# Attention and gated feed-forward on one core: three quarters of the layer norm on GpSimd, value tiles later, and the first products reordered

## The chip, the cores and the metric

The kernel runs on one core of one Trainium2 chip. The metric is device time in microseconds, the median of several runs; profiles show one execution each.

## The reference

The kernel computes a layer norm of `x` (2048 tokens of 512 values), and adds to `x` an attention block and a gated feed-forward block, both of the normalised tokens. There are 32 heads of 16 values.

```python
xn = _layernorm(x, axis=-1)
return x + _A_ref(xn, A_wqkv, A_wo) + _B_ref(xn, B_w1, B_w3, B_w2)
# _A_ref
    qkv = (x @ wqkv).reshape(B, S, 3, H, Dh) ...      # H = 32, Dh = 16
    scores = jnp.einsum("bhqd,bhkd->bhqk", q, k) * (Dh ** -0.5)
    p = _softmax(scores, axis=-1)
    o = jnp.einsum("bhqk,bhkd->bhqd", p, v)
    return o.transpose(...).reshape(B, S, D) @ wo
# _B_ref
    h = _silu(x @ w1) * (x @ w3)
    return h @ w2
```

## The kernel before

The 2048 queries are cut into four blocks of 512, the 32 heads into eight groups of four. A block and a group make one query tile `QT` (three buffers). Each is worked in units of 256 queries; the very last 256 queries are two units of 128. There are 65 units.

Each unit goes twice over its scores.

- The first pass finds the maximum of each query and head. TensorE makes a *product*: two matmuls (line 775, `p1_cand`) of 128 queries against 512 keys for two heads, which fill two of the PSUM banks 0 to 3. VectorE takes the maximum of 1024 columns (line 796, a *reduction*) into `part`. A unit of 256 queries has 16 products: four key blocks `kc`, two query tiles, two head pairs, key blocks outermost. Two bank pairs alternate, so TensorE can be at most two products ahead of VectorE. In all there are 1024 products. When a unit's last reduction is in, `final_max` (line 837) makes the negative maximum `negm`.
- GpSimd writes `negm` into two rows of `Z` (lines 813 and 815). For units in `FAST_AUG` the query tile is then built again by matmuls that include these rows (`tile_QT2`, copied by ScalarE at line 605). For all others three DMAs on SP carry the rows into `QT` (line 834, then line 830 twice). A unit that has this is "ready" (`AUG`).
- The second pass makes the scores again, transposed, with the maximum subtracted (line 904), and ScalarE takes the exponential of 512 columns (line 922) into a slot of `PT`. A unit of 256 queries has 32 of them, one of 128 queries 16. `tile_PV` multiplies by the values `Vaug`, whose 17th column of ones yields the sum; ScalarE copies the result to `U` (line 986), and a chain of DMAs and GpSimd operations divides by the sum (lines 1005 to 1031).

The feed-forward tiles and the output tiles are placed into what TensorE has left between these.

**The head.** `x` is fetched in four groups of four token tiles of 128 tokens (`load_x`, line 389) into `PT`, the weights `wk`, `wq` and `wv` by `load_w` (line 393) into `hT`. For each token group `ln_chunk` has VectorE take the statistics (lines 466 and 469) and GpSimd the inverse deviation `lnr` (line 474, and a power at line 476). The first group is normalised on VectorE (line 489). For the other three GpSimd also makes `lnb` = -mean times `lnr` (lines 480 and 482), and ScalarE normalises (line 494). A normalised tile lies in one of four slots of `osb`, is transposed on TensorE (line 518) and copied by ScalarE to `xnT` (line 524). With all four tiles of a group there, `tile_KT` makes 512 keys of the first head group (16 matmuls, copied at line 539), and `tile_QT` the first queries (copied at line 582). `tile_V` makes the values of one token tile (copied at line 558); there are 16 of these. The weights are spread out ("pads") with gaps of zeros: `wk` on GpSimd (lines 412 and 417), `wq` on ScalarE (lines 422 and 427). GpSimd also writes the ones of `Vaug` (line 440) and clears `wo` (line 442).

**What sets the order.** The order of instructions on each engine is fixed when the kernel is built. A planner keeps queues per engine (`dveq` and `redq` for VectorE, `expq` and `miscq` for ScalarE, `poolq` for GpSimd, `spq` for SP), a planned cost of each item (`occ`, `lat`) and the planned time at which each engine is free, and again and again emits the item that can start first. `pred` holds an item back until something is in `done`. TensorE tiles wait in `head_tiles`, `crit` (sorted by `need`, the number of the product before which the tile is wanted), `ffn` and `outs`; `assign` and `choose` give them one of the PSUM banks 4 to 7. `fill_cand` inserts matmuls whose result is not used where the planned load of TensorE in the last 2.3 us falls under a threshold. On the chip each engine follows the emitted order and waits on semaphores.

Of the kernel before, what the change touches and what calls it, by code (L numbers as in the profile page):

```python
# [225 lines left out]
def _build(nc, A_x, A_wqkv, A_wo, B_w1, B_w3, B_w2, out):  # L226
# [27 lines left out]
    for qc in range(NQC):  # L254
        for g in range(NG):
            last = qc == NQC - 1 and g == NG - 1
            for (q0, nq) in ([(0, 256), (256, 128), (384, 128)] if last else [(0, 256), (256, 256)]):
                units.append((qc, g, q0, nq))
    NU = len(units)
    FAST_AUG = {0, NU - 3, NU - 2, NU - 1}  # L260
    FAST_PV = {NU - 3, NU - 2, NU - 1}
# [4 lines left out]
    def sb(name, shape, dt):  # L266
        return ctx.enter_context(nc.sbuf_tensor(name, list(shape), dt))

    with ctx:
# [7 lines left out]
        lnr = sb("lnr", [128, NT], FP32)  # L277
        lnb = sb("lnb", [128, NT], FP32)
        lnt = sb("lnt", [128, NT], FP32)
# [112 lines left out]
        def load_w(dst, w, off):  # L392
            P.dma(lambda e: e.dma_start(dst, wqkv_v[:, :, off * D:(off + 1) * D]), writes=STG_KEYS[w], lat=5.0)
        load_x(0)
        load_w(wkst, "wk", 1)
        load_w(wqst, "wq", 0)
        load_x(1)
        load_x(2)
# [34 lines left out]
        for c in range(DC):  # L433
            poolq["pad"].append(_Item(pad_rest(wk, wkst, c), STG_KEYS["wk"], [("wk", 1 + c)], 0.62,
                                      pred=lambda: ("KT", 0, 0) in done))
        WK_KEYS = [("wkpad",)] + [("wk", i) for i in range(DC + 1)] + ON0_KEYS
# [3 lines left out]
        poolq["pad"].append(_Item(lambda e: e.memset(Vaug[:, :, :, 16:17], 1.0), [],  # L440
                                  [("Vone",)], 2.2))
        poolq["pad"].append(_Item(lambda e: e.memset(wo[:, :, :], 0.0), [], [("wo",)], 3.5,
# [18 lines left out]
        def ln_chunk(gi):  # L461
            tl = range(gi * XG, (gi + 1) * XG)
            sl_ = slice(gi * XG, (gi + 1) * XG)
            MVK = [("mv", t) for t in tl]
            for t in tl:
                dveq.append(_Item(lambda e, t=t: e.bn_stats(stats[:, t, :], x_sb[:, t, :]),
                                  [("PT", t)], [("st", t)], 0.6, 0.7))
            for t in tl:
                dveq.append(_Item(lambda e, t=t: e.bn_aggr(mv[:, t, :], stats[:, t, :]), [("st", t)], [("mv", t)],
                                  0.075, 0.2))  # L470

            def coef(op):
# [3 lines left out]
                q.append(_Item(lambda e: e.tensor_tensor(lnr[:, sl_], lnt[:, sl_], mhalf[:, sl_], ALU.pow),  # L476
                               [("lnt", gi), ("mhalf",)], [("lnr", gi)], 1.05, 1.15,
                               cb=norm if gi == 0 else None))
                if gi > 0:
                    q.append(_Item(lambda e: e.tensor_tensor(lnt[:, sl_], mv[:, sl_, 0], lnr[:, sl_], ALU.mult),  # L480
                                   [("lnr", gi)] + MVK, [("lnt", gi)], 0.25, 0.35))
                    q.append(_Item(lambda e: e.tensor_scalar(lnb[:, sl_], lnt[:, sl_], -1.0, 0.0, ALU.mult, ALU.add),
                                   [("lnt", gi)], [("lnb", gi)], 0.25, 0.35, cb=norm))

            def norm(op):
                for t in tl:
                    xs = t % 4
                    if gi == 0:
                        dveq.insert(t - gi * XG, _Item(lambda e, t=t, xs=xs: e.tensor_scalar(
                            xn_sb[:, xs, :], x_sb[:, t, :], mv[:, t, 0:1], lnr[:, t:t + 1], ALU.subtract, ALU.mult),  # L490
                            [("PT", t), ("lnr", gi), ("mv", t)], [("osb", xs)], 0.34, 0.45,
                            cb=lambda op, t=t: tr_ready(t)))
                    else:
                        miscq.append(_Item(lambda e, t=t, xs=xs: e.activation(  # L494
                            xn_sb[:, xs, :], x_sb[:, t, :], ACTF.Identity, scale=lnr[:, t:t + 1], bias=lnb[:, t:t + 1]),
                            [("PT", t), ("lnr", gi), ("lnb", gi)], [("osb", xs)], 0.55, 0.65,
                            cb=lambda op, t=t: tr_ready(t), pred=lambda t=t: ("xnT", t - 4) in done))
            dveq[-1].cb = coef
# [51 lines left out]
        def tile_V(t, need=None):  # L550
# [6 lines left out]
            def evac(bk):  # L557
                return [_Item(lambda e: e.activation(Vaug[:, t, :, 0:16],
                                                     bank(bk).rearrange("p (h d) -> p h d", d=16), ACTF.Identity),
                              [("ps", bk)], [("V", t)], _c_act(512), cb=lambda op: done.add(("V", t)))]  # L560
            return _Tile("V%d" % t, groups, evac, need=need, pred=lambda: ("xnT", t) in done)

# [179 lines left out]
        for u in range(NU):  # L742
            p1_first.append(len(p1))
            p1 += p1_list(u)
        NP1 = len(p1)
        p1_n = [0]
# [4 lines left out]
        def p1_cand():  # L751
# [19 lines left out]
            def emit():  # L771
# [328 lines left out]
        def assign():  # L1100
# [305 lines left out]
```

## Time and profile before

| what | value |
|---|---|
| median of three runs | 1257.77 us (1254.86 to 1262.67) |
| the profiled execution | 1256.76 us, its span 1255.0 us |
| VectorE busy | 1200.6 us, 96% |
| ScalarE busy | 1203.5 us, 96% |
| TensorE matmul busy | 1171.5 us, 93% |
| GpSimd busy | 358.7 us, 29% |
| normalising on ScalarE (line 494) | 12 operations, 8.9 us |
| value copies on ScalarE (line 558) | 16 operations, 9.4 us |
| first reduction | starts at 19.15 us |
| first exponential | starts at 51.83 us |
| last reduction | ends near 1215.2 us |
| last exponentials | 55 after the last query tile, ending near 1249.3 us |

Busy time is the time in which an engine runs at least one instruction. Consecutive instructions of one engine overlap a little, so the mean length of a group is above its busy time divided by its count. In the rows of groups the numbers behind the first bar are busy time in us and the mean length in ns; behind the second bar stands the time for which the engine was idle just before, and what ended it. A line number such as L456 can be that of a helper that makes many kinds of matmuls; the names of the tiles tell them apart.

### The profile page before, as it was taken

Reading aid. Unit: us, or ns where it says so; the run is one execution under the profiler, and the core shown is the slowest. Engines: PE = TensorE matmul, PEld = TensorE weight load, DVE = VectorE, ACT = ScalarE, POOL = GpSimd, SP = SyncE. Lnnn points to the kernel's source line nnn. Section 1 sums busy time; section 2 is a strip of 40 time slices with the busy share of each in tenths; the row PEclk is TensorE's granted clock in tenths of the full one; section 3 lists DMA queues with packets and bytes.
Section 4 is the critical chain, followed back from the end, with each engine's and each line's share of the span. In section 5 each row is a group of like instructions: output and inputs, shape, how many; then the busy total and the mean of one; then the engine's idle time right before and its main releaser. Section 6 shows DMA issues by size and latency. Waiting matters only on the chain.

```text
span 1255.0 us, 39328 instructions
## 1 busy us (share of the span) xinstructions
PE 1171.5 (93%) x16989; PEld 431.4 (34%) x16989; DVE 1200.6 (96%) x1141; ACT 1203.5 (96%) x2413; POOL 358.7 (29%) x453
## 2 busy tenths in 40 slices
PE   5999999999999999999999999999999999989997
PEld 2333333333333333333333333333333333333334
DVE  6999999999999999999999999999999999999972
ACT  6799999999999999999999999999999999999997
POOL 4023232232321133324322123333332115454110
PEclk9999999999999999999999999999999999998989
DMA  8010110111011011111110111111110112120000
GB/s 226 2 26 17 23 22 18 24 19 27 17 19 28 20 36 23 26 25 28 28 23 20 28 34 25 28 20 23 28 28 17 27 36 42 34 45 7 11 5 21
DMA packets 112845, 36.27 MB, mean 29 GB/s; under 512 B 98232, under 2 KB 112672, under 8 KB 112672
## 3 DMA queue, kind: packets, MB, share of 16 engines
q1 hardware_dynamic: 112672, 33.76, 12.6%
q8 instruction: 133, 2.18, 0.7%
q14 instruction: 40, 0.33, 0.1%
HBM read 22.81 MB, written 2.10 MB: 20 GB/s over the span
## 4 chain that ended last, share of the span: by engine, by line
PE 49%; ACT 48%; issue 1%; DVE 1%; DMA 1%; SPq 0%; ACTq 0%; POOL 0%
ACT PT L922 39%; PE ps L456 28%; PE ps L904 12%; PE ps L775 8%; ACT th L644 2%; ACT zg L646 2%; ACT ub L650 2%; ACT QT L582 1%; ACT KT L539 1%; DMA PT<-in_A_x_dram 1%; ACT U L986 1%; DVE part L796 0%; ACT osb L494 0%; ACT osb L707 0%; DVE R L975 0%
## 5 line engine op out<-in xcount | busy, mean ns | idle before, releaser
L796 DVE TENSOR_REDUCE part<-ps 128x2 f32<-128x1024 f32 x1024 | 1176.7, 1216 | 18.4 <-PE ps L775 10.1
L922 ACT ACTIVATE PT<-ps 128x512 bf16<-128x512 f32 x2048 | 1068.7, 636 | 24.8 <-PE ps L904 14.7
L904 PE MATMUL ps<-QT,KT 32*128 32x256 bf16 (+1 forms) x4160 | 565.1, 272 | 16.2 <-ACT QT L582 0.7
L775 PE MATMUL ps<-KT,QT 32*128 32x512 bf16 x2048 | 433.4, 385 | 2.0 <-DVE part L796 1.5
L904 PEld LDWEIGHTS ps<-QT,KT 32*128 32x128 bf16 x4160 | 182.1, 92 | 292.7 <-ACT PT L922 184.8
L1009 POOL TENSOR_TENSOR Rc<-Lc,mone 128x8 f32<-128x8 f32 x62 | 101.5, 1637 | 366.4 <-DMA Lc<-U 366.3
L456 PE MATMUL ps<-PT,Vaug 128*17 128x256 bf16 (+1 forms) x4160 | 178.5, 276 | 4.8 <-ACT PT L922 1.2
L456 PE MATMUL ps<-xnT,w 128*32 128x512 bf16 x1792 | 140.2, 384 | 25.8 <-ACT zg L646 21.0
L775 PEld LDWEIGHTS ps<-KT,QT 32*128 32x128 bf16 x2048 | 111.2, 91 | 145.4 <-issue 94.7
L456 PE MATMUL ps<-xnT,ident 128*32 128x512 bf16 x1732 | 138.8, 385 | 10.9 <-DVE osb L732 0.2
L456 PEld LDWEIGHTS ps<-PT,Vaug 128*17 128x17 bf16 x4160 | 83.4, 90 | 87.7 <-issue 65.0
L631 POOL TENSOR_TENSOR a<-zg,ub 128x512 f32<-128x512 bf16 x56 | 64.6, 1154 | 101.1 <-ACT ub L650 100.7
L813 POOL TENSOR_SCALAR Z<-negm 128x8 bf16<-128x8 f32 x64 | 14.7, 230 | 202.4 <-DVE negm L837 202.4
L633 POOL TENSOR_TENSOR hT<-a,t 128x512 bf16<-128x512 f32 x56 | 71.2, 1272 | 3.4
L456 PEld LDWEIGHTS ps<-xnT,w 128*32 128x32 bf16 x1792 | 39.3, 94 | 92.4 <-issue 74.9
L456 PE MATMUL ps<-w,hT 128*32 128x512 bf16 x896 | 70.6, 384 | 0.0
L456 PEld LDWEIGHTS ps<-xnT,ident 128*32 128x32 bf16 x1732 | 34.5, 94 | 83.3 <-ACT PT L922 70.1
L629 POOL TENSOR_SCALAR t<-th 128x512 f32<-128x512 bf16 x56 | 34.9, 623 | 55.6 <-ACT th L644 55.0
L456 PE MATMUL ps<-xnT,wq 128*32 128x512 bf16 (+2 forms) x576 | 43.2, 376 | 0.9 <-ACT zg L646 0.3
L456 PE MATMUL ps<-xnT,wk_on 128*32 128x512 bf16 x512 | 41.4, 400 | 1.7 <-ACT xnT L524 0.8
L1031 POOL TENSOR_TENSOR wk_on<-U,R 128x256 bf16<-128x256 f32 x30 | 21.9, 728 | 70.2 <-DMA R<-Rrow 69.9
L1031 POOL TENSOR_TENSOR on_b<-U,R 128x256 bf16<-128x256 f32 x32 | 23.3, 727 | 54.7 <-DMA R<-Rrow 54.7
(75 smaller groups left out, 432.1 us busy)
## 6 DMA issues: line engine op xcount, KB each, us to landing
w<-in_B_w_dram SPq DMA_DIRECT2D x112, 128.0 KB
R<-Rrow SPq DMA_DIRECT2D x248, 16.0 KB
PT<-in_A_x_dram SPq DMA_DIRECT2D x4, 512.0 KB
xr<-in_A_x_dram SPq DMA_DIRECT2D x16, 128.0 KB
out_dram<-osb SPq DMA_DIRECT2D x16, 128.0 KB
QT<-Zs SPq DMA_DIRECT2D x122, 2.0 KB
w<-in_B_w_dram SPq DMA_DIRECT2D x1, 1792.0 KB
hT<-in_A_wqkv_dram SPq DMA_DIRECT2D x3, 512.0 KB
```

The lines of the kernel that those rows point to most:

```text
L456: ins = e.matmul(bank(bk)[32 * i:32 * i + m, c0:c0 + ncols], make_lhsT(i), rhs_ap(i), start=start, stop=stop, tile_position=(0, 32 * i), **kw)
L629: q.append(_Item(lambda e: e.tensor_scalar(t1[:, :], th[:, ss, :], 1.0, 1.0, ALU.mult, ALU.add), [("th", ss)], [("t1",)], 0.62, 0.72))
L631: q.append(_Item(lambda e: e.tensor_tensor(a32[:, :], zg[:, ss, :], ub[:, ss, :], ALU.mult), [("zg", ss), ("ub", ss)], [("a32",)], 1.1, 1.25))
L633: q.append(_Item(lambda e: e.tensor_tensor(hT[:, fc, :], a32[:, :], t1[:, :], ALU.mult), [("a32",), ("t1",)], [("hT", fc)], 1.25, 1.35, cb ...
L644: return [_Item(lambda e: e.activation(th[:, ss, :], bank(bk), ACTF.Tanh, scale=0.5), [("ps", bk)], [("th", ss)], _c_act(512), cb=part_don ...
L646: _Item(lambda e: e.activation(zg[:, ss, :], bank(bk), ACTF.Identity, scale=0.5), [("ps", bk)], [("zg", ss)], _c_act(512), cb=part_done, n ...
L775: ins = e.matmul(bank(2 * sl + i), QT[32 * j:32 * j + 32, qs, q * 128:(q + 1) * 128], KT[32 * j:32 * j + 32, g, kc * 512:(kc + 1) * 512], ...
L796: redq.append(_Item(lambda e: e.tensor_reduce(part[:, par, qt, 2 * pair:2 * pair + 2, kc], ps[:, sl * 1024:(sl + 1) * 1024].rearrange("p ( ...
L904: ins = e.matmul(bank(b)[:, i * nq:(i + 1) * nq], KT[32 * j:32 * j + 32, g, (k0 + i) * 128:(k0 + i + 1) * 128], QT[32 * j:32 * j + 32, qs, ...
L922: expq.append(_Item(lambda e: e.activation(PT[:, sl, :], bank(b), ACTF.Exp, scale=SCALE), [("ps", b)], [("PT", sl)], _c_act(512), cb=cb))
L1009: poolq["nrm"].append(_Item(lambda e: e.tensor_tensor(Rc[:, pp, 0:nl], Lc[:, pp, 0:nl], mone[:, 0:nl], ALU.pow), [("Lc", pp), ("mone",)], ...
L1031: poolq["nrm"].append(_Item(lambda e: e.tensor_tensor(onorm[ob][:, g, q0:q0 + nq], U[:, us, 0:nq], R[:, pp, 0:nq], ALU.mult), [("U", us)] ...
```

## The change

- The first 256 queries of the first head group become two units of 128, and both are in `FAST_AUG`. There are now 66 units. The 16 products of these two units are put into this order: key block 0 for both units, key block 1 for both, then blocks 2 and 3 for the first unit, then for the second. A counter per unit (`p1_left`) tells when a unit's last reduction is in.
- `x` group 1 is fetched second, ahead of `wk` and `wq`.
- Token groups 1 to 3 are normalised on GpSimd, in the form that VectorE has for group 0: two per-partition scalars, subtract and multiply. `lnb` and its two operations are gone.
- Value tiles wait for the fourth key block of the first head group (`("KT", 0, NQC - 1)`). The rest of the `wq` pads waits for the same, the rest of the `wk` pads and the ones of `Vaug` for the last normalised tile. `tile_PV` waits for the last value tile.
- The `need` numbers of the query, key and value tiles change, and so do the conditions in `assign` and `fill_cand`.

```diff
@@ units
-            for (q0, nq) in ([(0, 256), (256, 128), (384, 128)] if last else [(0, 256), (256, 256)]):
+            first = qc == 0 and g == 0
+            for (q0, nq) in ([(0, 256), (256, 128), (384, 128)] if last else
+                             [(0, 128), (128, 128), (256, 256)] if first else [(0, 256), (256, 256)]):
...
-    FAST_AUG = {0, NU - 3, NU - 2, NU - 1}
+    FAST_AUG = {0, 1, NU - 3, NU - 2, NU - 1}
@@ loads
         load_x(0)
+        load_x(1)
         load_w(wkst, "wk", 1)
         load_w(wqst, "wq", 0)
-        load_x(1)
@@ pads of wk, ones of Vaug
-                                      pred=lambda: ("KT", 0, 0) in done))
+                                      pred=lambda: ("xn", NT - 1) in done))
...
-                                  [("Vone",)], 2.2))
+                                  [("Vone",)], 2.2, pred=lambda: ("xn", NT - 1) in done))
@@ ln_chunk, coef
-                               cb=norm if gi == 0 else None))
-                if gi > 0:
-                    q.append(_Item(lambda e: e.tensor_tensor(lnt[:, sl_], mv[:, sl_, 0], lnr[:, sl_], ALU.mult),
...
-                    q.append(_Item(lambda e: e.tensor_scalar(lnb[:, sl_], lnt[:, sl_], -1.0, 0.0, ALU.mult, ALU.add),
...
+                               [("lnt", gi), ("mhalf",)], [("lnr", gi)], 1.05, 1.15, cb=norm))
@@ ln_chunk, norm
+                    it = _Item(lambda e, t=t, xs=xs: e.tensor_scalar(
+                        xn_sb[:, xs, :], x_sb[:, t, :], mv[:, t, 0:1], lnr[:, t:t + 1], ALU.subtract, ALU.mult),
+                        [("PT", t), ("lnr", gi), ("mv", t)], [("osb", xs)], 0.34, 0.45,
+                        cb=lambda op, t=t: tr_ready(t))
                     if gi == 0:
...
+                        dveq.insert(t - gi * XG, it)
                     else:
-                        miscq.append(_Item(lambda e, t=t, xs=xs: e.activation(
-                            xn_sb[:, xs, :], x_sb[:, t, :], ACTF.Identity, scale=lnr[:, t:t + 1], bias=lnb[:, t:t + 1]),
...
+                        it.occ = 0.8
+                        it.lat = 0.9
+                        it.pred = lambda t=t: ("xnT", t - 4) in done
+                        poolq["ln"].append(it)
@@ tile_V
-            return _Tile("V%d" % t, groups, evac, need=need, pred=lambda: ("xnT", t) in done)
+            return _Tile("V%d" % t, groups, evac, need=need, pred=lambda: ("KT", 0, NQC - 1) in done)
@@ order of products
+        p1[0:16] = [b for kcs, us in (((0,), (0, 1)), ((1,), (0, 1)), ((2, 3), (0,)), ((2, 3), (1,)))
+                    for u in us for kc in kcs for b in p1_list(u) if b[2] == kc]
+        p1_left = [8 * units[u][3] // 128 for u in range(NU)]
...
-                    if red_n[0] == NP1 or p1[red_n[0]][0] != u:
+                    p1_left[u] -= 1
+                    if p1_left[u] == 0:
@@ due numbers
-            crit.append(tile_QT(ug, need=p1_first[2 * ug]))
+            crit.append(tile_QT(ug, need=32 * ug if ug > 1 else 20))
...
-                crit.append(tile_KT(g, sc, need=p1_first[2 * g] + 4 * sc))
+                crit.append(tile_KT(g, sc, need=32 * g + 4 * sc if g > 1 else 21 + 4 * sc))
...
-            crit.append(tile_V(t, need=24 + t))
+            crit.append(tile_V(t, need=12 + t))
@@ pv_ready
+            if ("V", NT - 1) not in done:
+                return False
@@ assign
-            if ("AUG", 0) not in done and p1_n[0] > 0 and not head_tiles:
+            if p1_left[0] > 1 and p1_n[0] > 0 and not head_tiles:
@@ fill_cand
-            if head_tiles or p1_n[0] < 48 or pv_u[0] >= NU or not low_load(P.free["pe"]):
+            if ("QT", 0) not in done or pv_u[0] >= NU or not low_load(P.free["pe"]):
@@ rest of the pads of wq
-                               pred=lambda: ("QT", 0) in done))
+                               pred=lambda: ("KT", 0, NQC - 1) in done))
```

More of the change, by code (lines that the diff above doesn't have):

```diff
@@ L277, in _build @@
         lnr = sb("lnr", [128, NT], FP32)
-        lnb = sb("lnb", [128, NT], FP32)
         lnt = sb("lnt", [128, NT], FP32)
@@ L476, in coef @@
                 q.append(_Item(lambda e: e.tensor_tensor(lnr[:, sl_], lnt[:, sl_], mhalf[:, sl_], ALU.pow),
-                               [("lnt", gi), ("mhalf",)], [("lnr", gi)], 1.05, 1.15,
-                               cb=norm if gi == 0 else None))
-                if gi > 0:
-                    q.append(_Item(lambda e: e.tensor_tensor(lnt[:, sl_], mv[:, sl_, 0], lnr[:, sl_], ALU.mult),
-                                   [("lnr", gi)] + MVK, [("lnt", gi)], 0.25, 0.35))
-                    q.append(_Item(lambda e: e.tensor_scalar(lnb[:, sl_], lnt[:, sl_], -1.0, 0.0, ALU.mult, ALU.add),
-                                   [("lnt", gi)], [("lnb", gi)], 0.25, 0.35, cb=norm))
+                               [("lnt", gi), ("mhalf",)], [("lnr", gi)], 1.05, 1.15, cb=norm))
             def norm(op):
@@ L487, in norm @@
                     xs = t % 4
+                    it = _Item(lambda e, t=t, xs=xs: e.tensor_scalar(
+                        xn_sb[:, xs, :], x_sb[:, t, :], mv[:, t, 0:1], lnr[:, t:t + 1], ALU.subtract, ALU.mult),
+                        [("PT", t), ("lnr", gi), ("mv", t)], [("osb", xs)], 0.34, 0.45,
+                        cb=lambda op, t=t: tr_ready(t))
                     if gi == 0:
[L489 to L492, printed above, removed]
-                    else:
-                        miscq.append(_Item(lambda e, t=t, xs=xs: e.activation(
-                            xn_sb[:, xs, :], x_sb[:, t, :], ACTF.Identity, scale=lnr[:, t:t + 1], bias=lnb[:, t:t + 1]),
-                            [("PT", t), ("lnr", gi), ("lnb", gi)], [("osb", xs)], 0.55, 0.65,
-                            cb=lambda op, t=t: tr_ready(t), pred=lambda t=t: ("xnT", t - 4) in done))
+                        dveq.insert(t - gi * XG, it)
+                    else:
+                        it.occ = 0.8
+                        it.lat = 0.9
+                        it.pred = lambda t=t: ("xnT", t - 4) in done
+                        poolq["ln"].append(it)
             dveq[-1].cb = coef
```

## The prediction

> **What bounds the kernel now.** I read the page first, then busy time by stretch, then the timelines of VectorE and ScalarE over the first 75 us, TensorE's over the first 53, and the last 60 us.
>
> ```profile
> PE 1171.5 (93%) x16989; PEld 431.4 (34%) x16989; DVE 1200.6 (96%) x1141; ACT 1203.5 (96%) x2413; POOL 358.7 (29%) x453
> ...
> L796 DVE TENSOR_REDUCE part<-ps 128x2 f32<-128x1024 f32 x1024 | 1176.7, 1216 | 18.4 <-PE ps L775 10.1
> L922 ACT ACTIVATE PT<-ps 128x512 bf16<-128x512 f32 x2048 | 1068.7, 636 | 24.8 <-PE ps L904 14.7
> ```
>
> Two engines are full at once: VectorE by 1024 reductions (L796), ScalarE by 2048 exponentials (L922). The stretches show where they are not (us, then busy us and count of PE, PEld, DVE, ACT, POOL; then the granted clock, the DMA share and GB/s):
>
> ```profile
> 19.00:33.20 14.20, 11.37 (x132) 4.91 (x132) 4.81 (x4) 14.20 (x26) 7.51 (x8) 0.76 0.53 119
> 33.20:51.83 18.63, 18.61 (x260) 6.78 (x257) 18.62 (x18) 10.58 (x20) 0.48 (x2) 1.00 0.01 3
> 51.83:73.00 21.17, 20.77 (x282) 7.13 (x278) 21.17 (x20) 21.05 (x42) 0.47 (x2) 1.00 0.07 16
> 110.00:400.00 290.00, 275.54 (x3922) 98.95 (x3924) 288.32 (x267) 286.55 (x579) 80.00 (x99) 1.00 0.11 21
> ```
>
> Between 19 and 33 us VectorE works 4.8 of 14.2 us while ScalarE has no gap: ScalarE holds up the head there. VectorE's timeline (start, length, count):
>
> ```profile
> 19.15 2.36 DVE L796 TENSOR_REDUCE part<-ps 128x2 f32<-128x1024 f32 x2 [0.19 <-PE ps L775]
> 22.51 1.23 DVE L796 TENSOR_REDUCE part<-ps 128x2 f32<-128x1024 f32 x1 [1.00 <-PE ps L775]
> 24.67 1.23 DVE L796 TENSOR_REDUCE part<-ps 128x2 f32<-128x1024 f32 x1 [0.93 <-PE ps L775]
> 33.20 14.80 DVE L796 TENSOR_REDUCE part<-ps 128x2 f32<-128x1024 f32 x13 [7.31 <-PE ps L775]
> 47.92 0.17 DVE L837 TENSOR_REDUCE negm<-part 128x8 f32<-128x32 f32 x1
> 48.02 18.18 DVE L796 TENSOR_REDUCE part<-ps 128x2 f32<-128x1024 f32 x16
> 66.12 0.17 DVE L837 TENSOR_REDUCE negm<-part 128x8 f32<-128x32 f32 x1
> ```
>
> The fifth reduction needs keys of the second token group (L539), and these come after twelve normalisations (L494, 8.9 us) and four value tiles (L558) on ScalarE. From 33.2 us on reductions follow each other at 14.80/13 = 1.14 us. The 33rd ends at 66.12.
>
> **Only the head can move.** I compared the order in which the two programs' instructions stand. From the 409th product (a pair of L775 matmuls feeding one reduction) and the 751st exponential on, every engine has the same instructions in the same order, the tail with its 55 last exponentials included. So the gain is how much earlier the two full engines arrive there, and VectorE cannot arrive earlier by more than it idles before.
>
> **The change part by part.**
>
> *Loads.* Token group 1 is fetched second. By the old landings (5.15, 6.70, 8.15, 9.65 us: first reader of each fetch) it lands at 6.7, wk at 8.15, wq at 9.65. GpSimd does the wk pad first: 8.15 + 0.41 + 0.20 (L474) + 1.02 (L476) + gaps = 9.9, so the first normalisation starts 0.35 earlier than at 10.26. Statistics end at 18.6, not 18.95; first reduction at 18.8. wq's pad at 9.65 + 0.42 stays ahead of its matmuls near 15.
>
> *Normalising on GpSimd.* ScalarE loses 8.9 us. GpSimd gains twelve 512-element operations, which no row shows; nearest are:
>
> ```profile
> L629 POOL TENSOR_SCALAR t<-th 128x512 f32<-128x512 bf16 x56 | 34.9, 623 | 55.6 <-ACT th L644 55.0
> L633 POOL TENSOR_TENSOR hT<-a,t 128x512 bf16<-128x512 f32 x56 | 71.2, 1272 | 3.4
> ```
>
> One tensor input costs 0.62 (0.57 for 448 in L417), two cost 1.15 to 1.27. It reads one tensor and two per-partition scalars, so I take 0.65 and keep 0.57 and 1.27. A group then takes 0.2 + 1.0 + 0.15 + 4 x 0.65 = 4.0 us, below the 4.56 of the four reductions it must stay ahead of. Normalising would run from 14.8 to about 25.4. Then pads 4 x 0.57, ones 2.38 (L440) and the clearing of wo 3.51 (L442) end at 33.8, before the first maximum at about 35.6, which GpSimd must pass on (L813); that cover is 1.8 us, gone at 0.80 per normalisation. At 1.27 group 3 ends at 17.5 + 12 x 1.27 = 32.7, its keys exist 2.8 later (transpose, xnT 0.6, KT matmuls 0.98, KT copy 0.7), at 35.5, and VectorE, which would need them at 32.1, loses 3.4. The Trainium skill (GPSIMD Engine Reference, section 3.1) says 512 elements take about 769 ns in the best loop and that elementwise work belongs on VectorE; here L489 shows 0.34 on VectorE against 0.62. By 0.77 a group takes 4.4 us, still below 4.56, and the sum stays.
>
> *Value tiles wait, units of 128, products in key order.* Of the first 16 products four need group 0 only, four group 1. Ideal: 18.8 + 33 x 1.137 + 0.1 for one more L837 = 56.4, so 9.7 earlier than 66.12. What is late instead: TensorE. These rows show two rates:
>
> ```profile
> 26.55 2.01 PE L518 MATMUL ps<-ident,osb 128*128 128x128 bf16 x12 [1.60 <-ACT osb L494]
> 28.49 1.90 PE L456 MATMUL ps<-xnT,wk_on 128*32 128x512 bf16 x16
> ...
> 33.33 1.04 PE L456 MATMUL ps<-xnT,wk_on 128*32 128x512 bf16 x16
> ```
>
> Sixteen matmuls took 1.90 and then 1.04. In the new order the four transposes of group 1, a filling group and 12 of the 16 KT matmuls stand before the third product. Products 1 and 2 go at 17.45. Slowly the rest takes 4 x 0.6, then 0.6 for the xnT copy, 0.43 and 1.3: product 3 ends near 22.8, its reduction is wanted at 21.1, loss 1.7; fast it ends near 21.4, loss 0.3. The old trace turned fast only at 19.04, after 5.6 us of unbroken matmuls; the new order has a gap at 16.6, so I take slow for this group and fast after it. With 0.2 for later joins: 1.9. After product 3 a fast TensorE needs per group 0.98 + 4 x 0.28 + 0.23 + 4 x 0.32 = 3.6, under 4.56. V tiles of 16 matmuls with a product between take 0.98 + 0.32 = 1.30, against 1.14, but two products are ready ahead.
>
> The skill (TensorE: Matmul & The Clock Gate, section "What's actually happening") would have the clock fall only after a whole idle window of about 3.4 us and rise after one busy window, at a phase that varies by run. The trace disagrees on the fall: a gap of 1.6 us (24.95 to 26.55) was followed by the slow rate. By the rule the loss would stay between 0.3 and 1.9.
>
> *First exponential.* Old: maximum at 47.92, exponential at 51.83. New: the 13th reduction ends at 18.8 + 14.8 + 1.9 = 35.5; product 16 stands before the query tile, which puts the exponential near 39.2. From there ScalarE has 32 exponentials x 0.513 (10.77/21), 8 V copies x 0.49, KT, QT and QT2 1.3 = 21.6 us, while 18 reductions take 20.5: with so little spare, 0.7 lost. V copies once hidden in ScalarE's gaps now lie among exponentials.
>
> *Sum.* The 33rd reduction ends at 56.4 + 1.9 + 0.7 = 59.0: VectorE gains 7.1. Unit 2 (256 queries) still goes through three DMAs on SP (old: maximum 66.12, transpose issued 66.96, rows 69.37 to 70.60, landed by about 72.4, so first exponential possible 6.6 after the maximum). New: 59.0 + 6.6 = 65.6, where the old 33rd exponential started at 73.2; but four KT copies (0.57 each) and a QT copy (0.47) are then still undone, 2.75 us. ScalarE is ahead by 7.6 - 2.75 = 4.9. It can make up the other 2.2 from its own idle time (3.45 us between 110 and 400) or not. I take the middle, 6.0. Hidden at no cost: the moved pads (L417 ends near 27.7 on GpSimd, L427 is done on ScalarE before 35; their first readers stand behind products 24 and 27, near 47 us and later); the wo loads (L447) that SP issues behind the clearing of wo, at 33.9 instead of 25.3, with the next SP work, unit 2's transpose, at 59.6; the extra 128-query normalising round on SP and GpSimd (SP mostly waits), two more small ScalarE copies 0.5 (in ScalarE's spare before unit 2).
>
> The profiled execution took 1256.76 for its span of 1255.0. Less 6.0 is 1250.8; the same off the median 1257.77 is 1251.8. I forecast 1251.3.
>
> **The rivals.**
> 1. *VectorE's whole gain.* TensorE is fast from the second group on and ScalarE recovers: 9.7 - 0.3 = 9.4, so 1248. For: ScalarE idled 1.2% between 110 and 400. Against: the gap at 16.6. Chance 0.15.
> 2. *GpSimd is dear, or ScalarE loses more.* At 1.27 per normalisation 6.0 - 3.4 = 2.6 remain, 1254.7; the same if 18 reductions run 3.4 us behind ScalarE's exponentials instead of 0.7. For: ScalarE had 0.12 us of idle in 51.83 to 73. Against: one tensor input. The gain would be gone at 1.48 per normalisation. Chance 0.17.
> 3. *Slower: TensorE stays at the slow rate until product 16.* Per group 1.7 + 4 x 0.54 + 0.43 + 4 x 0.33 = 5.6 against 4.56, then five V tiles at 1.7: product 16 ends near 45.4, the 33rd reduction near 66.3. VectorE gains nothing, and ScalarE, with 2.75 still undone at 66.3 + 6.6 = 72.9, is 2.4 late: 1257.3 + 2.4 = 1259.7. It decides where the slow rate lasts past product 13. For: the slow rows from 26.55 to 33. Against: unbroken matmuls turned fast after 5.6 and 4.6 us, and the new order is denser. Chance 0.10.
>
> **How the numbers follow.** Forecast 0.58, rivals 0.15, 0.17, 0.10. The forecast's own range is 1249 to 1254. Three runs spread from 1254.86 to 1262.67, so a median can be off by 2; the range for 8 in 10 reaches from just below rival 1 to between rivals 2 and 3: 1246.5 to 1258. One per cent is 12.6 us, about what a measurement of this kernel can tell from no change. No case reaches it: a gain is capped by VectorE's idle time at 9.7. Scatter leaves 0.06 for faster, 0.04 for slower, 0.90 for within.
>
> **What would show it.** Right: first reduction near 18.8, no L796 wait over 2 us behind it, 33rd reduction ending between 57 and 61, first L922 near 39, a ScalarE gap of 2 to 4 us before unit 2, normalising on POOL at 0.6 to 0.8 ending near 26, last reduction some 6 us before 1215. Wrong: POOL above 1 us each; L456 groups of 16 at 1.9 after 25 us; VectorE gaining 7 but the end less than 4.

## The result: slower by 0.75%

| | before | changed |
|---|---|---|
| median | 1257.24 us (1253.88 to 1262.67) | 1266.41 us (1263.46 to 1273.56, 9 runs) |
| ratio of times, 95% interval | | 1.0075 [1.005, 1.010] |
| profiled execution | 1256.76 us, span 1255.0 us | 1264.04 us, span 1262.1 us |
| first reduction starts | 19.15 us | 18.34 us |
| 33rd reduction ends | 66.12 us | 74.48 us |
| last `negm` | 1215.21 us | 1222.71 us |

The forecast was 1251.3 us with a range of 1246.5 to 1258. The measured time is slower than before and outside the range, though within the 1% to which the forecast gave 0.90. The times of the last `negm` say where it was lost: 8.4 us at the 33rd reduction, 7.5 at the last one, 7.1 in the span. The whole loss is made in the head and carried to the end.

In the tables further down, executions over 1.5% slower than the fastest of their kernel (two of e_act near 1272 us, one of e_only_ma at 1278) stand in the medians and not in the ratios.

The page of the changed kernel (the same rows as before) shows little of this. VectorE is as busy as before, and ScalarE 8.0 us less, mostly by the normalisations that it no longer does. The idle time of L796 has grown from 18.4 to 26.3 us, with the part that products end (L774) up from 10.1 to 19.0. What points at the cause is GpSimd: it is busy 24.1 us longer (358.7 before), where twelve normalisations at the forecast price would add 7.8:

```profile
PE 1174.0 (93%) x17097; PEld 438.1 (35%) x17097; DVE 1200.7 (95%) x1142; ACT 1195.5 (95%) x2403; POOL 382.8 (30%) x463
...
L796 DVE TENSOR_REDUCE part<-ps 128x2 f32<-128x1024 f32 x1024 | 1177.3, 1216 | 26.3 <-PE ps L774 19.0
L922 ACT ACTIVATE PT<-ps 128x512 bf16<-128x512 f32 x2048 | 1069.4, 639 | 22.9 <-PE ps L904 14.0
```

The timeline of VectorE shows where most of these 19 us lie (start, length, count, and in brackets the idle time before and what ended it):

```profile
18.34 2.31 DVE L796 TENSOR_REDUCE part<-ps 128x2 f32<-128x1024 f32 x2
26.29 1.23 DVE L796 TENSOR_REDUCE part<-ps 128x2 f32<-128x1024 f32 x1 [5.63 <-PE ps L774]
...
34.41 1.23 DVE L796 TENSOR_REDUCE part<-ps 128x2 f32<-128x1024 f32 x1 [3.43 <-PE ps L774]
...
43.61 1.23 DVE L796 TENSOR_REDUCE part<-ps 128x2 f32<-128x1024 f32 x1 [2.89 <-PE ps L774]
47.90 3.49 DVE L796 TENSOR_REDUCE part<-ps 128x2 f32<-128x1024 f32 x3 [3.07 <-PE ps L774]
...
74.48 0.17 DVE L837 TENSOR_REDUCE negm<-part 128x8 f32<-128x32 f32 x1
```

There is a long wait at each token group. The releaser named is TensorE, but TensorE itself waits. Its transposes (L514) come one tile at a time, 2.06 us apart, and the timeline of GpSimd says why:

```profile
22.95 0.61 PE L514 MATMUL ps<-ident,osb 128*128 128x128 bf16 x4 [1.45 <-POOL osb L483]
```

```profile
14.64 8.25 POOL L483 TENSOR_SCALAR osb<-PT,mv,lnr 128x512 bf16<-128x512 bf16 x4
...
24.38 8.24 POOL L483 TENSOR_SCALAR osb<-PT,mv,lnr 128x512 bf16<-128x512 bf16 x4
...
34.12 8.24 POOL L483 TENSOR_SCALAR osb<-PT,mv,lnr 128x512 bf16<-128x512 bf16 x4
42.33 2.17 POOL L418 TENSOR_SCALAR wk_on<-hT 128x448 bf16<-128x448 bf16 x4
```

Four normalisations take 8.25 us, 2.07 each, where 0.65 was forecast. GpSimd starts a group every 9.74 us, and the four reductions of a group take 4.56. In busy time by stretch the stretch from 19 to 33.2 us, which the change was to fill, has VectorE at 5.34 of 14.20 us (before: 4.81), TensorE at 8.12 (before: 11.37), and GpSimd at 13.76:

```profile
19.00:33.20 14.20, 8.12 (x54) 3.07 (x52) 5.34 (x5) 4.18 (x8) 13.76 (x10) 1.00 0.26 80
33.20:51.83 18.63, 15.76 (x139) 4.86 (x138) 10.06 (x10) 7.90 (x14) 17.07 (x12) 1.00 0.03 9
```

### The profile page after: what moved, and what is told of

Read it like the earlier page. It is cut to its first block, busy times and chain, and to the rows that moved or that the text cites. A ratio compares the mean times of both kernels' runs of the same rounds, so it can differ in the third digit from the quotient of the medians.

```text
span 1262.1 us, 39574 instructions
## 1 busy us (share of the span) xinstructions
PE 1174.0 (93%) x17097; PEld 438.1 (35%) x17097; DVE 1200.7 (95%) x1142; ACT 1195.5 (95%) x2403; POOL 382.8 (30%) x463
## 4 chain that ended last, share of the span: by engine, by line
ACT 47%; PE 44%; DVE 4%; POOL 2%; issue 1%; DMA 1%; SPq 0%; ACTq 0%; POOLq 0%
ACT PT L922 39%; PE ps L457 25%; PE ps L904 11%; PE ps L774 8%; DVE part L796 3%; ACT th L640 2%; ACT zg L642 2%; POOL osb L483 2%; ACT ub L646 2%; ACT QT L578 1%; ACT KT L535 1%; ACT U L986 1%; DMA hT<-in_A_wqkv_dram 0%; POOL lnr L477 0%; DMA Zs<-Z 0%
## 5 line engine op out<-in xcount | busy, mean ns | idle before, releaser
L796 DVE TENSOR_REDUCE part<-ps 128x2 f32<-128x1024 f32 x1024 | 1177.3, 1216 | 26.3 <-PE ps L774 19.0
L774 PE MATMUL ps<-KT,QT 32*128 32x512 bf16 x2048 | 440.6, 387 | 2.1 <-ACT QT L578 0.7
L904 PEld LDWEIGHTS ps<-QT,KT 32*128 32x128 bf16 x4224 | 186.3, 92 | 290.2 <-ACT PT L922 183.9
L1009 POOL TENSOR_TENSOR Rc<-Lc,mone 128x8 f32<-128x8 f32 (+1 forms) x63 | 101.8, 1616 | 335.5 <-DMA Lc<-U 335.3
L774 PEld LDWEIGHTS ps<-KT,QT 32*128 32x128 bf16 x2048 | 114.0, 91 | 146.4 <-issue 99.7
L813 POOL TENSOR_SCALAR Z<-negm 128x8 bf16<-128x8 f32 (+1 forms) x65 | 14.8, 227 | 197.0 <-DVE negm L837 197.0
L629 POOL TENSOR_TENSOR hT<-a,t 128x512 bf16<-128x512 f32 x56 | 71.2, 1271 | 3.6
L1031 POOL TENSOR_TENSOR on_b<-U,R 128x256 bf16<-128x256 f32 (+1 forms) x33 | 23.4, 710 | 83.1 <-DMA R<-Rrow 83.1
```

The source lines that it names most:

```text
L629: q.append(_Item(lambda e: e.tensor_tensor(hT[:, fc, :], a32[:, :], t1[:, :], ALU.mult), [("a32",), ("t1",)], [("hT", fc)], 1.25, 1.35, cb ...
L774: ins = e.matmul(bank(2 * sl + i), QT[32 * j:32 * j + 32, qs, q * 128:(q + 1) * 128], KT[32 * j:32 * j + 32, g, kc * 512:(kc + 1) * 512], ...
L796: redq.append(_Item(lambda e: e.tensor_reduce(part[:, par, qt, 2 * pair:2 * pair + 2, kc], ps[:, sl * 1024:(sl + 1) * 1024].rearrange("p ( ...
L904: ins = e.matmul(bank(b)[:, i * nq:(i + 1) * nq], KT[32 * j:32 * j + 32, g, (k0 + i) * 128:(k0 + i + 1) * 128], QT[32 * j:32 * j + 32, qs, ...
L1009: poolq["nrm"].append(_Item(lambda e: e.tensor_tensor(Rc[:, pp, 0:nl], Lc[:, pp, 0:nl], mone[:, 0:nl], ALU.pow), [("Lc", pp), ("mone",)], ...
L1031: poolq["nrm"].append(_Item(lambda e: e.tensor_tensor(onorm[ob][:, g, q0:q0 + nq], U[:, us, 0:nq], R[:, pp, 0:nq], ALU.mult), [("U", us)] ...
```

## The experiments

Theory 1: the price of one normalisation on GpSimd is the whole miss, and every other step of the sum holds. What makes it dear was open at first: two per-partition scalars (A), the pair of operations (B), or other engines at the same memory (C). Rivals to theory 1: the new order of products, the late value tiles or the later pads cost something themselves.

| label | what differs | median | ratio to before | 33rd reduction ends |
|---|---|---|---|---|
| e_const | changed kernel, constants, subtract and multiply | 1265.99 | 1.008 [1.0046, 1.0115] | 73.47 |
| e_const_ma | changed kernel, constants, multiply and add | 1252.62 | 0.9961 [0.9936, 0.9986] | 58.95 |
| e_muladd | changed kernel, `x * lnr + lnb` on GpSimd, planned anew | 1260.57 | 1.0039 [1.0012, 1.0065] | 62.49 |
| e_muladd0 | the same in the changed kernel's order | 1254.95 | 0.9970 [0.9946, 0.9994] | 63.79 |
| e_addmul | changed kernel, `(x + nmean) * lnr` on GpSimd | 1251.36 | 0.9956 [0.9929, 0.9983] | 61.27 |
| e_act | changed kernel, ScalarE normalises | 1255.41 | 0.9981 [0.9961, 1.0001] | 61.66 |
| e_only_ma | kernel before, GpSimd normalises with `x * lnr + lnb` | 1263.02 | 1.0072 [1.004, 1.0103] | 66.52 |
| e_dve | changed kernel, VectorE normalises | 1261.68 | 1.0030 [1.0009, 1.005] | 68.38 |
| e_dve2 | the same, GpSimd's pads after it | 1254.21 | 0.9977 [0.9958, 0.9996] | 62.56 |

The executions of one kernel spread over 6 to 15 us (e_const_ma: 1246.34 to 1258.51), so the last column, read from one profile, says which mechanism works, and the ratio says what it is worth.

### What makes a GpSimd `tensor_scalar` dear

`m1_forms` is a kernel of its own that issues each form three times; `m2_pairs` does the same for pairs of operations.

> A kernel of its own that computes none of the reference: GpSimd runs forms of one tensor_scalar on 128x512 bf16, three of each, while the other engines are still, then VectorE and ScalarE run the same form. In the changed kernel one normalisation took 2.07 us on GpSimd; the nearest old rows (two constants) took 0.57 to 0.62. Theory A (the two per-partition scalars are what costs): two constants 0.65, one per-partition scalar about 1.3, two about 2.07, whatever the pair of operations. Theory B (the pair subtract, multiply costs): 2.07 also with two constants subtract, multiply, and about 0.65 for multiply, add with two per-partition scalars. Theory C (VectorE's work beside it costs): here, with VectorE still, about 0.65 for all. The 256- and 64-element forms tell a fixed cost from one per element: if it is per element, 1.1 and 0.35.

Rows of its page (busy us and mean ns behind the bar). L248 is two constants, multiply and add; L250 two constants, subtract and multiply; L252 a per-partition scalar and a constant, subtract and multiply; L256 two per-partition scalars, subtract and multiply, the form of the changed kernel; L258 two per-partition scalars, multiply and add.

```profile
L248 POOL TENSOR_SCALAR o<-x_sb 128x512 bf16<-128x512 bf16 x3 | 1.9, 621 | 7.8 <-DMA x_sb<-in_A_x_dram 7.6
L256 POOL TENSOR_SCALAR o<-x_sb,sc 128x512 bf16<-128x512 bf16 x3 | 6.2, 2076 | 0.3
...
L252 POOL TENSOR_SCALAR o<-x_sb,sc 128x512 bf16<-128x512 bf16 x3 | 6.0, 1995 | 0.3
L250 POOL TENSOR_SCALAR o<-x_sb 128x512 bf16<-128x512 bf16 x3 | 5.8, 1925 | 0.2
...
L258 POOL TENSOR_SCALAR o<-x_sb,sc 128x512 bf16<-128x512 bf16 x3 | 2.3, 772 | 0.3
```

It costs 2076 ns with all other engines silent, so C falls. Two per-partition scalars with multiply and add cost 772 ns, and two constants with subtract and multiply 1925 ns, so A falls and B stands: per-partition scalars add 0.15 us, the pair adds 1.30.

> A kernel of its own that computes none of the reference: GpSimd runs tensor_scalar on 128x512 bf16 with two per-partition scalars and different pairs of operations, three of each; then VectorE runs eight of its normalisations beside GpSimd's clearing of 4096 bf16 (3.8 us) and four alone. If a fast form exists for multiply, add only: 0.77 for that pair, about 2 for the other four pairs. If every pair that begins with multiply is fast: about 0.8 for multiply, subtract and multiply, multiply too. If subtract is what is slow: add, multiply fast. On VectorE: 0.35 to 0.41 alone; if GpSimd's work stretches it, near 1.8 as beside the pads, else 0.4 throughout.

All with per-partition scalars: L251 multiply, add; L252 multiply, subtract; L253 add, multiply; L254 subtract, multiply; L255 multiply, multiply.

```profile
L251 POOL TENSOR_SCALAR o<-x_sb,sc 128x512 bf16<-128x512 bf16 x3 | 2.3, 769 | 7.7 <-DMA x_sb<-in_A_x_dram 7.7
L254 POOL TENSOR_SCALAR o<-x_sb,sc 128x512 bf16<-128x512 bf16 x3 | 6.2, 2097 | 0.0
L252 POOL TENSOR_SCALAR o<-x_sb,sc 128x512 bf16<-128x512 bf16 x3 | 6.2, 2090 | 0.0
...
L255 POOL TENSOR_SCALAR o<-x_sb,sc 128x512 bf16<-128x512 bf16 x3 | 2.3, 792 | 0.0
L253 POOL TENSOR_SCALAR o<-x_sb,sc 128x512 bf16<-128x512 bf16 x3 | 2.3, 782 | 0.0
```

Whether the addition or the multiplication stands first makes no difference. Every pair here with a subtract, in either place, costs 2.1 us; every pair without one, 0.77 to 0.79.

### The price alone, in the kernel

```diff
@@ e_const: norm, groups 1 to 3
+                        it.fn = lambda e, t=t, xs=xs: e.tensor_scalar(
+                            xn_sb[:, xs, :], x_sb[:, t, :], 0.0, 20.0, ALU.subtract, ALU.mult)
@@ e_const_ma
...
+                            xn_sb[:, xs, :], x_sb[:, t, :], 20.0, 0.0, ALU.mult, ALU.add)
```

> The changed kernel, but groups 1 to 3 are normalised on GpSimd with two constants in place of mean and inverse deviation; the order of instructions on every engine is that of the changed kernel. Leaves out the layer norm of three quarters of the tokens. Theory 1 (the price of the normalisation alone made the change slower, the rest of the prediction's sum holds): a normalisation takes 0.65, the keys of group 3 are copied near 29 instead of 45.7, the 33rd reduction ends near 59, the time is 1249 to 1254. Theory 2 (TensorE's slow rate in the head is a cause of its own): matmul groups of 16 stay at 1.7 to 1.9 until product 13, the 33rd reduction ends at 64 to 66, the time is 1256 to 1260. Theory 3 (the later value tiles and the units of 128 cost ScalarE more than they bring): the 33rd reduction ends near 59, but the time is 1256 or more.

Constants did not make it cheap: 1924 ns each, as B has it, and the time stayed that of the changed kernel. The expectation of a cheap operation was A's, and missed.

> As the run with constants, but in the order multiply, add (0.62 us alone on GpSimd, where subtract, multiply took 1.93 with constants); every engine has the changed kernel's instructions in the changed kernel's order. Leaves out the layer norm of three quarters of the tokens. Theory 1 (the price of the normalisation alone; the rest of the prediction's sum holds): the keys of group 3 are copied near 29 to 31, the 33rd reduction ends near 59, the time is 1249 to 1254. Theory 2 (TensorE's slow rate in the head costs by itself): groups of 16 matmuls stay at 1.7 to 1.9 until product 13, the 33rd reduction ends at 64 to 66, 1256 to 1260. Theory 3 (value tiles among the exponentials and the 128-query units cost more than they bring): the 33rd reduction ends near 59 but the time is 1256 or more.

All five engines have the changed kernel's instructions in its order; only the price of twelve operations differs. Timelines of GpSimd and of VectorE:

```profile
14.59 2.72 POOL L490 TENSOR_SCALAR osb<-PT 128x512 bf16<-128x512 bf16 x4
```

```profile
22.30 9.38 DVE L798 TENSOR_REDUCE part<-ps 128x2 f32<-128x1024 f32 x8 [1.67 <-PE ps L776]
32.60 3.49 DVE L798 TENSOR_REDUCE part<-ps 128x2 f32<-128x1024 f32 x3 [0.92 <-PE ps L776]
...
58.95 0.18 DVE L839 TENSOR_REDUCE negm<-part 128x8 f32<-128x32 f32 x1
```

At 0.68 each, the 33rd reduction ends at 58.95 us, 15.5 before the changed kernel's. The first exponential starts at 39.24 and unit 2's at 65.83 us. The medians lie 13.8 us apart. This is theory 1. That 58.95 is so near to the forecast 59.0 is in part luck: the profiled execution is the fastest of its twelve (1246.34 us), and TensorE turned fast early in it, as the next runs show.

### A cheap form of the same normalisation

```diff
@@ e_muladd: lnb and its two operations are back; norm, groups 1 to 3
...
+                            xn_sb[:, xs, :], x_sb[:, t, :], lnr[:, t:t + 1], lnb[:, t:t + 1], ALU.mult, ALU.add)
@@ e_muladd0: the same, and the two operations that make lnb are planned at no cost
+                                   [("lnr", gi)] + MVK, [("lnt", gi)], 0.0, 0.0))
...
+                        poolq["ln"].insert(t - gi * XG, it)
@@ e_addmul: nmean = -mean, one operation per group, planned at no cost
+                    q.append(_Item(lambda e: e.tensor_scalar(nmean[:, sl_], mv[:, sl_, 0], -1.0, 0.0, ALU.mult, ALU.add),
+                                   MVK, [("nmean", gi)], 0.0, 0.0))
...
+                            xn_sb[:, xs, :], x_sb[:, t, :], nmean[:, t:t + 1], lnr[:, t:t + 1], ALU.add, ALU.mult)
```

> The changed kernel with the whole layer norm, normalising on GpSimd as x times lnr plus lnb (multiply, add with two per-partition scalars, 0.77 alone) with the two small operations for lnb back; the planner orders anew. A group takes GpSimd 0.2 + 1.0 + 0.2 + 0.2 + gaps 0.3 + 4 x 0.8 = 5.1 us, the last normalisation ends near 28.5 instead of 42.4. Theory 1: 33rd reduction near 59 to 60, time 1250 to 1255. Theory 2: 64 to 66 and 1257 or more. Theory 3: near 60 but 1256 or more.

Missed. The normalisations were cheap, but the two small operations per group moved the planner's times, and up to about the 800th product it put the instructions in another order. Until the 33rd reduction VectorE was 3.6 us early (62.49). By the 49th, after waits of 1.35 and 2.02 us, that was gone (84.24 against 84.46). Six operations of 0.2 us are too short for this; the order that they caused is left, and the next run holds it fixed.

> The whole layer norm with multiply, add on GpSimd as in the run before, but with the two small operations planned at no cost, so that every engine has the changed kernel's order (GpSimd with six small operations more). A group takes GpSimd 5.0 instead of the 4.2 of the constants. If the price was all that made the change slower, and the run before with multiply, add lost its gain through its own other order: the 33rd reduction ends at 59 to 61 and the time is 1251 to 1255, a ratio to the kernel before of 0.994 to 0.999. If the two small operations and the dearer form lose it: 62 or later and a ratio of 1.000 or more. If the 128-query units and the late value tiles lose it (theory 3): near 60 but a ratio of 1.000 or more.

With the order held, the ratio is 0.9970 [0.9946, 0.9994], against 1.0039 [1.0012, 1.0065]: it was the order. The 33rd reduction, at 63.79, came later than expected, though GpSimd was done in time (28.71). The timelines of TensorE say why: e_const_ma first, then e_addmul, e_muladd0 and e_muladd0_b:

```profile
17.19 0.40 PE L776 MATMUL ps<-KT,QT 32*128 32x512 bf16 x4 [0.71 <-ACT QT L580]
...
23.89 0.39 PE L776 MATMUL ps<-KT,QT 32*128 32x512 bf16 x2
```

```profile
17.25 0.61 PE L781 MATMUL ps<-KT,QT 32*128 32x512 bf16 x4 [0.70 <-ACT QT L585]
...
28.61 0.60 PE L781 MATMUL ps<-KT,QT 32*128 32x512 bf16 x2
...
30.02 0.39 PE L781 MATMUL ps<-KT,QT 32*128 32x512 bf16 x2
```

```profile
33.53 0.61 PE L784 MATMUL ps<-KT,QT 32*128 32x512 bf16 x2
34.34 1.79 PE L458 MATMUL ps<-xnT,wk_on 128*32 128x512 bf16 x16 [0.21 <-ACT xnT L530]
...
37.02 0.40 PE L784 MATMUL ps<-KT,QT 32*128 32x512 bf16 x4
```

```profile
34.05 1.90 PE L458 MATMUL ps<-xnT,wk_on 128*32 128x512 bf16 x16 [0.21 <-ACT xnT L530]
...
39.50 0.39 PE L784 MATMUL ps<-KT,QT 32*128 32x512 bf16 x2
```

Four executions with the same TensorE instructions in the same order: the pair of a product takes 0.39 us from 23 us on, or only from 30, 36 or 38. (In e_const_ma TensorE was fast at 17.19 already, and slow again between 20 and 23.) The 33rd reduction follows: 58.95, 61.27, 63.79, 64.55.

> The changed kernel, where GpSimd normalises groups 1 to 3 as (x + nmean) * lnr, with add and multiply in place of subtract and multiply; nmean = -mean is one small GpSimd operation per group more. All other instructions stand in the order of the changed kernel. Theory (the price of subtract is the whole loss): 0.78 per normalisation, four in 3.1, the last one ends near 28 us; first reduction 18.4; if TensorE runs fast after product 3, the 33rd reduction ends between 59 and 60.5 and the last maximum near 1207, ratio 0.994 to 0.998. If TensorE stays slow through the head, as in the profile of the version with multiply and add and lnb, the 33rd ends near 63.5 with waits of about 2 us at 23 and 37. Rival (the order of products or the later value tiles cost something that GpSimd's lateness hid): no better than 1.002 although GpSimd is cheap.

The slow rate lasted until 29 us in its profile, and the 33rd reduction ended at 61.27, between the two cases expected. The ratio 0.9956 [0.9929, 0.9983] lies where theory 1 had it: about 5.5 us faster than before and the lowest median of all kernels here. The rival, that order and late value tiles cost as much as they bring, is excluded.

> The same kernel as the version with multiply and add and lnb planned at no cost, profiled once more. In its first profile TensorE's groups ran at the slow rate from 20.7 to 35 us, and the 33rd reduction ended at 63.79. If the slow rate depends on the execution, this profile may show 16 L458 matmuls in about 1.05 before 30 us and the 33rd reduction near 60; if it follows from this kernel's own gaps, the groups are slow until 35 again and the 33rd reduction ends within 0.5 of 63.8.

One more execution of e_muladd0: slow until 37.6 us, 33rd reduction at 64.55. The rate did not turn before 30 us; one execution does not exclude that the moment varies.

The traces settle a part of it. Up to 17.2 us TensorE has the same matmuls, at the same times within 0.03 us, in the changed kernel, e_const, e_const_ma, e_addmul and e_muladd0_b. The four matmuls that follow took 0.40 us in e_const and e_const_ma, and 0.61 in the other three. Between e_const and the changed kernel GpSimd's work up to there is alike too. So what the kernel feeds TensorE does not alone set the first turn; this speaks for the execution. What sets how long the slow rate lasts behind it stays open.

### Other engines for the normalisation, and the normalisation alone

```diff
@@ e_act: miscq has ScalarE's form of before, lnb is back; and, which neither kernel has:
-            for k, it in enumerate(miscq[:6]):
+            for k, it in enumerate(miscq[:24] if ("KT", 0, NQC - 1) not in done else miscq[:6]):
@@ e_only_ma, in the kernel before
-                        miscq.append(_Item(lambda e, t=t, xs=xs: e.activation(
+                        poolq["ln"].append(_Item(lambda e, t=t, xs=xs: e.tensor_scalar(
+                            xn_sb[:, xs, :], x_sb[:, t, :], lnr[:, t:t + 1], lnb[:, t:t + 1], ALU.mult, ALU.add),
```

> The changed kernel with one part undone: groups 1 to 3 are normalised on ScalarE as before (with the two small GpSimd operations for the bias); the planner orders anew. A group then takes ScalarE 4 x 0.73 + 4 x 0.5 + 0.57 = 5.5 us against the 4.56 of four reductions. Theory 1: the 33rd reduction ends near 61 to 62, ScalarE does 8.9 us more than in the changed kernel but in its idle head, the time is 1251 to 1255. Theory 2: near 66, 1258 or more. Theory 3: near 61 but 1258 or more.

The rest of the change, with the old engine, brings the 33rd reduction to 61.66 us, 4.5 earlier than before; the ratio, 0.9981 [0.9961, 1.0001], is at most a small gain. More than the engine was put back: the planner also looked at 24 items of ScalarE's `miscq` in place of 6 until the first keys are made. With that, product order and late value tiles do no harm.

> The kernel before with one part of the change alone, at the low price: groups 1 to 3 normalised on GpSimd as multiply, add; value tiles, units of 256 and the order of products and loads as before. ScalarE loses 8.9 us in the head. If moving the normalisation is the part that brings the gain, the keys of group 1 come 4 or more earlier than 30.4 and the time is 1250 to 1254; if the later value tiles and the units of 128 are needed for it, the 33rd reduction stays past 63 and the time is 1255 or more.

Alone, the move to GpSimd brings nothing even when it is cheap. In the old GpSimd queue the ones of `Vaug` and the clearing of `wo` stand ahead of it:

```profile
18.75 2.56 POOL L440 MEMSET Vaug<- 128x512 bf16 x1
...
21.07 3.02 POOL L494 TENSOR_SCALAR osb<-PT,lnr,lnb 128x512 bf16<-128x512 bf16 x4
...
24.42 3.51 POOL L442 MEMSET wo<- 128x4096 bf16 x1
...
29.47 6.08 POOL L494 TENSOR_SCALAR osb<-PT,lnr,lnb 128x512 bf16<-128x512 bf16 x8
```

Groups 2 and 3 end at 35.55 us, and the 33rd reduction at 66.52. That this queue is the reason is argued, not tested alone: value tiles and units, too, are those of before. Its profile explains some 2 us (last `negm` 1217.43 against 1215.21); why its median is 5.5 above is not settled.

```diff
@@ e_dve: VectorE normalises all groups
...
-                        poolq["ln"].append(it)
+                        dveq.insert(t - gi * XG, it)
@@ e_dve2: the same, and the rest of the wk pads waits for the last normalised tile
+            poolq["pad"].append(_Item(pad_rest(wk, wkst, c), STG_KEYS["wk"] + [("osb", 3)], [("wk", 1 + c)], 0.62,
```

> The changed kernel with groups 1 to 3 normalised on VectorE, 0.35 apart each as for group 0: 12 x 0.35 = 4.2 us more on VectorE in the head, nothing on ScalarE or GpSimd; the planner orders anew. Theory 1: the 33rd reduction ends near 61 to 62 (56.4 + 4.2 + small joins), the time is 1250 to 1254. Theory 2: near 66, 1257 or more. Theory 3: near 62 but 1257 or more.

It missed on a cost that no theory had. Three groups of four normalisations took 1.38 or 1.39 us on VectorE, the fourth 7.37, while GpSimd wrote pads, ones and `wo` (first fence: VectorE; second: GpSimd):

```profile
25.23 7.37 DVE L483 TENSOR_SCALAR osb<-PT,mv,lnr 128x512 bf16<-128x512 bf16 x4
```

```profile
24.42 2.24 POOL L418 TENSOR_SCALAR wk_on<-hT 128x448 bf16<-128x448 bf16 x4
26.61 2.43 POOL L441 MEMSET Vaug<- 128x512 bf16 x1
28.64 3.81 POOL L443 MEMSET wo<- 128x4096 bf16 x1
```

> The version with VectorE normalising, where four normalisations took 7.37 us instead of 1.38 while GpSimd made pads and cleared tiles; here GpSimd's pads wait for the last normalisation, one wait more, nothing else. If it was GpSimd's work at the same time that stretched them, they take 1.4 again, the 33rd reduction ends near 62.4 instead of 68.4 and the time falls by about 6, to 1253 to 1257. If the length has another cause, it stays near 7.4 and the time near 1261.

With GpSimd's work moved behind the fourth group, the same four take 1.37 us, the 33rd reduction ends 5.8 us earlier (62.56 for 68.38), and the median falls by 7.5:

```profile
25.24 1.37 DVE L483 TENSOR_SCALAR osb<-PT,mv,lnr 128x512 bf16<-128x512 bf16 x4
```

## Why the prediction was wrong

**The step that failed** is the price of a normalisation, "so I take 0.65 and keep 0.57 and 1.27". It measured 2.07, above the upper bound. Both rows that gave 0.62 and 0.57 (L629 and L417) are multiply-and-add; that can be read in the code at those lines. The rows were matched by the number of tensor inputs, and the pair of operations was not matched. No `tensor_scalar` row of before had a subtract on GpSimd (its one subtract there is L815, a `tensor_tensor` of 8 columns), so the upper bound, a two-input operation, bounded another thing. The Trainium skill's 769 ns (GPSIMD Engine Reference, section 3.1), set beside the rows in the forecast, is what multiply and add measured (769 and 772); for a subtract it is too low by a factor of 2.7.

**The formula around it held.** With 2.07 in "group 3 ends at 17.5 + 12 x 1.27", in place of the 1.27, it gives 42.3 us; the last normalisation ended at 34.12 + 8.24 = 42.36. With 2.8 more its keys exist at 45.1, VectorE wanted them at 32.1, and the loss is 13.0: 6.0 of gain become 7.0 of loss. The profiled execution lost 7.3. Rival 2 was this mechanism and named 1.48 as the point where the gain is gone; it was priced only to 1.27, and so ended at 1254.7.

**The other steps held at the price assumed.** e_const_ma, at 0.68, in its fastest execution (the last row has medians):

| step | forecast | e_const_ma | changed kernel |
|---|---|---|---|
| first reduction starts | 18.8 | 18.32 | 18.34 |
| wait ahead of the third reduction | 1.7 | 1.67 | 5.63 |
| 33rd reduction ends | 59.0 | 58.95 | 74.48 |
| first exponential | 39.2 | 39.24 | 54.77 |
| unit 2's first exponential | 65.6 | 65.83 | 81.36 |
| time against before | -6.0 | 1252.62 - 1257.53 = -4.9 | +9.2 |

**One step held only sometimes:** "slow for this group and fast after it" for TensorE. It was so in e_const_ma; in e_addmul and e_muladd0 the wait ahead of the third reduction was 2.3 us and the slow rate went on. In the changed kernel TensorE, fed one tile at a time, took 1.90 us for the 16 matmuls of the last keys at 43.71, which is part of the 2.5 us by which the 33rd reduction is later than 59.0 + 13.0. In e_muladd0 the slow rate lasted into the last keys without starvation: rival 3 in part, with a 33rd reduction 4.8 us later than e_const_ma's. Against rival 3 the forecast had set that unbroken matmuls turned fast after 5.6 and 4.6 us. The first fast pairs of the old trace stand a little earlier, at 18.72 and 32.77 us, which makes 5.2 and 4.3; but e_muladd0_b shows that such a time is no bound. Even there the 33rd reduction comes 9.9 us before the changed kernel's (64.55 against 74.48), so the slow rate changes the size of the gain and not the cause of the miss.

## What to carry to other kernels

Before moving an operation to another engine, find a row with the same pair of operations, the same kinds of scalars and the same size; where there is none, the bound is open, and the number to give is the price at which the gain is gone. Write a normalisation on GpSimd as `(x + (-mean)) * r`: the minus sign made once on a column costs 0.2 us, a subtract in each tile 1.3. And what a queue does after the moved work matters as much as the work: in the old queue, behind the `Vaug` ones, a cheap normalisation brought nothing, and beside GpSimd's pads and clearing four of VectorE's own took five times as long.

## What the runs showed of the hardware that was not expected

- **GpSimd's `tensor_scalar` with a subtract** costs 1.93 to 2.10 us for 512 elements per partition, 1.22 for 256 and 0.58 for 64: about 0.37 us and 3.3 ns per element. Without a subtract it is 0.62 (constants) to 0.79. bf16 and f32 cost the same (2076 ns).
- **VectorE's `tensor_scalar` on 512 bf16 is held up while GpSimd clears a tile.** In m2_pairs eight of them started beside one clearing of 4096 elements (3.55 us) and took 5.74; four alone took 1.38:

```profile
36.18 5.74 DVE L262 TENSOR_SCALAR d<-x_sb,sc 128x512 bf16<-128x512 bf16 x8 [36.18 <-POOL sc L266]
42.18 1.38 DVE L262 TENSOR_SCALAR d<-x_sb,sc 128x512 bf16<-128x512 bf16 x4 [0.26 <-POOL sc L269]
```

  Eight alone would take 2.76, so the clearing cost 3 us, nearly its own length. They are not all slowed: the first took 3.48 us and ended at 39.66, just behind the clearing (39.52), and the others took 0.40 each. In e_dve it was likewise the last of the four, from 26.73 to 32.59 us, which waited out both fillings (to 32.45); the three beside the pads took 0.46 to 0.64. The Trainium skill (GPSIMD Engine Reference, section 1, Specifications) says that the two engines share their SBUF interfaces and that some VectorE modes contend; it gives no size. The trace agrees and gives one.
- **TensorE's slow rate can outlast steady work.** In e_muladd0_b it worked from 19.2 to 37.6 us with no pause over 0.3 us and stayed slow. The Trainium skill (TensorE: Matmul & The Clock Gate, section "What's actually happening") would have it fast after one busy window of about 3.4 us; the measurement differs.
- **The granted clock of a stretch can read 1.00 while TensorE is slow.** It is 1.00 in the changed kernel's stretch from 19 to 33.2 us, where every group was slow. The first record of that clock in the trace lies at 48.36 us; in e_const_ma it lies at 16.31, in e_addmul at 29.07, in e_muladd0 at 35.88 and in e_muladd0_b at 37.98, each where the groups turn fast, and a stretch ahead of it reads 1.00. Behind it the clock does show the slow rate: 0.50 from 19.8 to 23.1 us in e_const_ma and from 25.6 to 32.3 in the kernel before. Within each trace the changes lie whole multiples of 3.41 us apart (e_const_ma: 16.31, 19.73, 23.14).
